# Attention and two feed-forward layers on one core: raw-weight loads one half-step nearer to their first use, and the third block's attention re-timed

## The chip, the cores and the metric

The kernel runs on one core of a Trainium2 chip. The metric is the device time of one execution in microseconds (us), smaller is better. The engines are PE (TensorE matmul; PEld its weight loads), DVE (VectorE), ACT (ScalarE), POOL (GpSimd) and SP (SyncE, which here only issues transfers).

## The reference, cut to what matters

```python
scores = (q @ k^T) / 8                 # 4 batches, 8 heads, 576 tokens, head size 64
# heads 0-3: a query sees its last 32 keys; heads 4-7: every 4th key of its last 128
attn = softmax(where(mask, scores, -1e9))
x = (attn @ v) as (2304 tokens, 512)
h = x @ w_in                           # 512 x 2048
y = where(h > 0, h, exp(min(h, 0)) - 1) @ w_out
out = ((y @ w_a) * (y @ w_b)) @ w_out2 # 512 x 1536, 1536 x 512
```

All inputs are float32, and the weights reach the core as raw 64-bit words (two halves each), from which the kernel assembles the float32 number with some vector work.

## The kernel before, in words

**Two stages.** The tokens are cut into six blocks `t` = 0 to 5 of 384. The first stage computes the first feed-forward layer in 96 steps; a step `s` is one (block, 128-column chunk of w_in) pair from the list `STEPS1`: steps 0 to 6 are block 0, 7 to 22 block 1, 23 to 31 the rest of block 0, and from 32 on 16 steps for each of blocks 2 to 5. The second stage computes the second layer in twelve big steps (`ab_step`, L974 and L1290).

**One step.** In the main loop (`for s in range(NS1)`) a step runs, in this order: slot L (transfers), `h1_mm(s)` (12 matmuls of w_in, L525, then the negated relu and the exp of it on ACT, L546 and L547), slots A0 and A, `h1_g(s)` (DVE joins the two, L552; ACT and POOL split the result in a high and a low part, L536 and L537), slot C, `y1_mm(s - 2)` (12 matmuls of w_out, L571), slots B, B2, B3, C2. So the second product follows its own first product by two steps. `ps_h`, the result of L525, has two buffers, so `h1_mm(s)` needs L552 of step `s - 2` to be done.

**Attention, block by block.** A block's four head pairs `p` (0, 1 plain, 2, 3 dilated) are computed some steps before the block's own steps: q and k are loaded (`att_load`, L335, three buffers `qk`), then v (`att_load_v`, L349, two buffers), then scores (`att_scores`, L474: both heads' results in the two buffers of the PSUM pool `ps_a`), softmax of head 0 and of head 1 one step later (mask added by DVE L490, maximum L356, exp on ACT L360, scaled by POOL L370), transposes (`att_transpose`, L499, each into a `ps_a` buffer, copied out by ACT, L502), and the product with v (`att_values`, L514, again a `ps_a` buffer; ACT L462 and DVE L463 make `x` of it). Which step each happens in is a table: `B1` for block 1, `B2` for block 2, and a formula for the later ones; `end` is the step of the transposes. Block 2 is the third block.

**Background work.** The rest of w_in and w_out and all weights of the second layer are assembled from raw words between the steps: `unit_ops` and `chunk_ops` list operations (`Op`), and `tick`, called twice a step (slots C and A0: a half-step), hands out those that are ready, within a room for each engine. A chunk is loaded (`load`, L866, into one of four `wraw` buffers), then ACT runs `high` and `low` (L252, L257), DVE the rest (L262, L267, L270), DVE forms sums (L917), ACT and DVE split them (L278, L901), and SP and ACT store them to DRAM (L829), from which the second stage fetches them (L651). `Op.ready` (L773) holds an operation back until those before it were handed out some half-steps ago. For the first operation on a loaded chunk this is `LAG_IN`; `first` is true in the first 32 half-steps (steps 7 to 22), and from half-step `LATE` = 146 (step 80) on `LAG_LATE` = 7 holds:

```python
C1, C0, AHEAD, LAG_IN, LAG_OUT = SPLIT, NF1 + SPLIT, 56, 4, 2
...
                    lag = LAG_IN - first if now[0] < LATE else LAG_LATE
                    lag = lag if x.takes else 2
```

The order of instructions on an engine is fixed when the program is built. ACT, DVE, POOL and SP run theirs one after another, so an operation that waits holds up all behind it.

Of the kernel before, what the change touches and what calls it, by code (L numbers as in the profile page):

```python
# [22 lines left out]
B, H, S, D = 4, 8, 576, 64  # L23
# [8 lines left out]
NP = H // 2  # L32
KC = DM // 128
NF1, NF2 = F1 // 128, F2 // 128


SPLIT = 7
# [13 lines left out]
Y2_LAG = 6  # L51


C1, C0, AHEAD, LAG_IN, LAG_OUT = SPLIT, NF1 + SPLIT, 56, 4, 2
LATE, LAG_LATE = 2 * (NF1 * (NB - 1) - C1), 7

ROOM1 = {"V": 1.8, "A": 1.4, "G": 0.9}
# [6 lines left out]
ON3 = {"a": ("AV",) * 4, "b": ("AV",) * 4, "o": ("AV",) * 4}  # L64
CV0, CV1, LAG = 3, 8, 3
B1 = (-4, -2, 0, 2)
B2 = (18, 21, 23, 26)
EARLY = 2
UE = {False: (64, 6), True: (48, 8)}
LP, LD = TB + WIN, NU * UK  # L70
# [145 lines left out]
def banded_attention_two_ffn(ctx: ExitStack, tc: tile.TileContext, ins, out):  # L216
    nc = tc.nc
    V, A, G, T, SP = nc.vector, nc.scalar, nc.gpsimd, nc.tensor, nc.sync
# [366 lines left out]
    def y1_mm(s):  # L585
        for part in y1_parts(s):
            part()
# [117 lines left out]
    def y2_steps(S):  # L705

        first, rest = [], []
        for op, i in (("11", 0), ("21", 1)):
            first += [(y2_tiles, S, op), (y2_load, S, op, i, 0)]
        first += [(int,)] * Y2_LAG  # L710
        for op in ("11", "21"):
            first.append((y2_split, S, op, "AA", "VV"))
        rest += [(y2_temp, S, "t3"), (y2_load, S, "t3", 0, 1)]
        rest += [(y2_tiles, S, "22"), (y2_load, S, "22", 1, 1)]
        rest += [(y2_temp, S, "t1"), (y2_load, S, "t1", 0, 0)]
        rest += [(y2_sum, S, "t1", "t3", "t1")]
        rest += [(y2_temp, S, "t2"), (y2_sum, S, "t2", "22", "t1")]
        rest += [(y2_tiles, S, "t2"), (y2_split, S, "t2", "AA", "VV")]
        rest += [(y2_tiles, S, "t1"), (y2_split, S, "t1", "AA", "VV")]
        rest += [(y2_sum, S, "t3", "22", "t3")]  # L720
        rest += [(y2_temp, S, "t4"), (y2_load, S, "t4", 1, 0)]
        rest += [(y2_tiles, S, "t3"), (y2_split, S, "t3", "AA", "VV")]
        rest += [(y2_sum, S, "t4", "t4", "t2")]
        rest += [(y2_tiles, S, "t4"), (y2_split, S, "t4", "AA", "VV")]
        rest += [(y2_split, S, "22", "AA", "VV"), (y2_t.clear,)]
        return first, rest
# [39 lines left out]
    ops, room, now = [], {"A": 0.0, "V": 0.0, "G": 0.0}, [0]  # L766
    n_free = {"wraw": NRAW, "wt": 4}

    class Op:
# [6 lines left out]
        def ready(self):  # L776
            for x in self.after:
                if x.at is None:
                    return False
                first = now[0] <= 2 * (C0 - C1)  # L780
                if x.eng == "D":
                    lag = LAG_IN - first if now[0] < LATE else LAG_LATE
                    lag = lag if x.takes else 2
                elif self.gives and first:
                    lag = 0
                elif self.eng == "D":
                    lag = self.lag if self.fn else 1
                else:
                    lag = int(x.eng != self.eng)
                if x.at + lag > now[0]:  # L790
                    return False
            if self.takes and n_free[self.takes] <= 0:
                return False
            return self.eng == "D" or room[self.eng] >= 0
# [527 lines left out]
    def at_step(step, slot, fn, *args):  # L1322
        todo.setdefault((step, slot), []).append((fn, args))

    def run(step, slot):
        for fn, args in todo.pop((step, slot), ()):
            fn(*args)
# [25 lines left out]
    first = steady.tile([128, 4], F32, "nm")  # L1353
# [17 lines left out]
    for i in range(len(seq) + 4):  # L1371
        if i < len(seq):
            p, b = seq[i]
# [9 lines left out]
        if 0 <= i - LAG < len(seq):  # L1383
            p, b = seq[i - LAG]
# [28 lines left out]
    for t in range(1, NB):  # L1413
        for p in range(NP):
            if t == 1:
                b0 = B1[p]
            elif t == 2:
                b0 = B2[p]
            else:
                b0 = NF1 * (t - 1) - 4 + 4 * p  # L1420
            at_step(max(0, b0 - 3), "L", held, att_load, t, p)
            at_step(max(0, b0 - 3) if t < EARLY else b0 + 2, "L", held, att_load_v, t, p)
            if t < EARLY:
                end = b0 + 1 + int(b0 >= 0)
                at_step(max(b0, 0), "A", early_scores, t, p)
                for i in range(2):
                    at_step(max(b0 + i, 0), "A", early_softmax, t, p, i)
                    at_step(max(end + i, 0), "B", early_transpose, t, p, i, A)
                at_step(max(end + 2, 0), "B2", early_values, t, p)
            else:  # L1430
                at_step(b0, "A", att_scores, t, p)
                hurry = t == EARLY and p == NP - 1
                end = b0 + 4 + int(not hurry)
                for i in range(2):
                    at_step(b0 + i, "A", att_softmax, t, p, i)
                    at_step(end, ("B", "B2")[i] if hurry else ("A", "B")[i], att_transpose, t, p, i, A)
                at_step(end + 1, "B2" if hurry else "B", att_values, t, p)
    at_step(6, "L", lambda: SP.dma_start(out=masks, in_=ins["masks"]))

    at_step(NF1 + 13, "L2", held, y_part_load)  # L1440
# [49 lines left out]
    first, rest = y2_steps(0)  # L1490
# [5 lines left out]
    for s in range(NS1):  # L1496
# [7 lines left out]
        if s >= 2:  # L1504
            y1_mm(s - 2)
        for sl in ("B", "B2", "B3", "C2"):
            run(s, sl)
# [68 lines left out]
```

## Time and profile before

| what | value |
|---|---|
| time, median of 3 runs | 928.32 us (927.14 to 930.19) |
| the profiled execution | 928.17 us |
| its span, first to last instruction | 926.3 us |
| busy: PE, PEld, DVE | 903.6, 864.9, 650.9 us |
| busy: ACT, POOL | 522.8, 288.1 us |
| DMA queues q1 and q10 | 55.5% and 5.6% of 16 engines' span |
| L525, L571, L974, L1290 on PE | 224.0, 225.1, 294.1, 154.1 us |

The time and the span differ by 1.9 us of start and end. PE's busy time is counted from the start of a matmul to a modelled end, so two matmuls in a row overlap, and a busy PE can still run below its best rate: what a group takes is read from its start to the start of the next group. "Idle before" in a row is time in which the engine stood still, with what ended it.

### The profile page before, as it was taken

To read this page: it belongs to the slowest core of one execution; us is meant where nothing else is said; L and a number is where in the kernel's file an instruction comes from. 1 tells how busy PE (TensorE), PEld (TensorE's weight loads), DVE (VectorE), ACT (ScalarE), POOL (GpSimd) and SP (SyncE) were. 2 spreads that over 40 slices of the span, in tenths; PEclk is the share of its full clock that TensorE was granted. 3 is DMA by queue.
4 is the path that set the end of the run, shared out by engine and by line. 5 is a ranking of instruction groups with operands and counts; after the bars stand their busy time and mean duration, and the time that the engine had idled before them with its cause. 6 is when DMAs were issued, how large, how long until landed. Compare 5 with 4: busy or idle time off the path is not lost. (4 is left out here: it accounts for less than half of the span.)

```text
span 926.3 us, 17004 instructions
## 1 busy us (share of the span) xinstructions
PE 903.6 (98%) x6155; PEld 864.9 (93%) x6157; DVE 650.9 (70%) x1147; ACT 522.8 (56%) x1328; POOL 288.1 (31%) x260
## 2 busy tenths in 40 slices
PE   9999997999999999999999999999999999999998
PEld 5789987999999999999998999999999999999998
DVE  6898898758656767666775258788746688746566
ACT  6897787776777776776566354224343325342331
POOL 2323233323333323342232132222622222622233
PEclk9999998999999999999999999999999999999999
DMA  9854443557455554535897489884687663686622
GB/s 282 239 207 171 138 154 118 200 157 245 149 173 165 198 179 164 182 137 187 297 345 275 171 278 346 270 302 157 212 336 268 241 224 117 227 324 242 238 70 69
DMA packets 75859, 195.79 MB, mean 211 GB/s; under 512 B 8288, under 2 KB 22240, under 8 KB 75776
## 3 DMA queue, kind: packets, MB, share of 16 engines
q1 hardware_dynamic: 63680, 175.70, 55.5%
q10 hardware_dynamic: 12096, 19.01, 5.6%
q8 instruction: 49, 0.80, 0.3%
q14 instruction: 34, 0.28, 0.1%
HBM read 151.16 MB, written 43.52 MB: 210 GB/s over the span
## 5 line engine op out<-in xcount | busy, mean ns | idle before, releaser
L974 PE MATMUL ps_h<-y,w 128*128 128x384 f32 x1512 | 294.1, 337 | 2.5 <-DVE el L1029 1.1
L974 PEld LDWEIGHTS ps_h<-y,w 128*128 128x128 f32 x1512 | 255.9, 188 | 6.6 <-DVE el L1029 2.0
L525 PE MATMUL ps_h<-x,w 128*128 128x384 f32 x1152 | 224.0, 341 | 5.5 <-DVE el L552 3.9
L571 PE MATMUL ps_y<-g,w 128*128 128x384 f32 x1152 | 225.1, 341 | 3.2 <-ACT w L278 1.4
L525 PEld LDWEIGHTS ps_h<-x,w 128*128 128x128 f32 x1152 | 198.5, 188 | 12.9 <-DVE el L552 6.5
L571 PEld LDWEIGHTS ps_y<-g,w 128*128 128x128 f32 x1152 | 200.4, 189 | 8.4 <-ACT el L608 1.8
L537 POOL TENSOR_TENSOR g<-el,g 128x384 fp32r<-128x384 f32 x96 | 118.7, 1236 | 276.8 <-ACT g L536 236.6
L1290 PE MATMUL ps_o<-w,g 128*128 128x256 f32 x1071 | 154.1, 282 | 0.4 <-ACT g L1090 0.4
L1290 PEld LDWEIGHTS ps_o<-w,g 128*128 128x128 f32 x1071 | 147.4, 188 | 1.3 <-ACT g L1090 0.9
L552 DVE SCALAR_TENSOR_TENSOR el<-el,ps_h 128x384 f32<-128x384 f32 x96 | 52.9, 551 | 90.3 <-ACT el L547 89.6
L1016 POOL TENSOR_TENSOR g<-el,g 128x384 fp32r<-128x384 f32 x34 | 39.4, 1160 | 120.5 <-ACT g L1015 105.6
L1313 DVE TENSOR_TENSOR acc<-acc,ps_o 128x512 f32<-128x512 f32 (+1 forms) x77 | 49.6, 644 | 32.0 <-PE ps_o L1290 31.6
L536 ACT ACTIVATE g<-el 128x384 fp32r<-128x384 f32 x96 | 49.9, 520 | 28.6 <-DVE el L552 27.1
L546 ACT ACTIVATE el<-ps_h 128x384 f32<-128x384 f32 x96 | 46.3, 482 | 33.6 <-PE ps_h L525 27.2
L370 POOL TENSOR_TENSOR e<-e,rs 96x512 f32<-96x512 f32 (+2 forms) x40 | 40.3, 1007 | 54.7 <-DVE rs L369 44.0
L267 DVE SCALAR_TENSOR_TENSOR wt<-wt,wraw 128x512 uint32<-128x512 uint32 x68 | 53.9, 796 | 2.8 <-ACT wraw L257 1.3
L270 DVE SCALAR_TENSOR_TENSOR wt<-wraw,wt 128x512 uint32<-128x512 uint32 x68 | 53.9, 798 | 0.6
L547 ACT ACTIVATE el<-el 128x384 f32<-128x384 f32 x96 | 50.2, 523 | 1.6
L257 ACT ACTIVATE wraw<-wraw 128x512 uint32<-128x512 uint32 x68 | 44.8, 668 | 10.4 <-DMA wraw<-in_w2b 6.9
L360 ACT ACTIVATE e<-e,nm 96x128 f32<-96x128 f32 x128 | 49.8, 392 | 1.5 <-ACT nm L358 1.0
L252 ACT ACTIVATE wt<-wraw 128x512 f32<-128x512 f32 x68 | 44.8, 665 | 5.4 <-DMA w2Q__5915<-wt 2.0
L1064 DVE TENSOR_TENSOR u<-ps_h,u 128x384 f32<-128x384 f32 x36 | 20.0, 556 | 36.2 <-PE ps_h L974 36.2
(111 smaller groups left out, 1071.0 us busy)
## 6 DMA issues: line engine op xcount, KB each, us to landing
w<-w2P_o SPq DMA_DIRECT2D x52, 512.0 KB, 5.6
w<-w2P_a SPq DMA_DIRECT2D x48, 512.0 KB, 4.5
w<-w2P_b SPq DMA_DIRECT2D x48, 512.0 KB, 4.3
wraw<-in_w1i SPq DMA_DIRECT2D x16, 512.0 KB, 4.3
wraw<-in_w1o SPq DMA_DIRECT2D x16, 512.0 KB, 3.3
wraw<-in_w2a SPq DMA_DIRECT2D x12, 512.0 KB, 3.6
wraw<-in_w2b SPq DMA_DIRECT2D x12, 512.0 KB, 4.2
wraw<-in_w2o SPq DMA_DIRECT2D x12, 512.0 KB, 4.2
```

The costliest lines, as they stand in the source:

```text
L267: V.scalar_tensor_tensor(t, t, 3, L, op0=ALU.logical_shift_left, op1=ALU.bitwise_or)
L270: V.scalar_tensor_tensor(t, H, 0x80000000, t, op0=ALU.bitwise_and, op1=ALU.bitwise_or)
L360: A.activation(e[:, i], sc[:, i], AF.Exp, bias=nm[:, i : i + 1], scale=scale, accum_out=sm[:, i : i + 1],)
L525: T.matmul(ps[:, :TB], w[:, wi, kc * 128 : (kc + 1) * 128], xs[kc][:, xi, :], start=(n == 0), stop=(n == 3 * KC - 1),)
L536: A.activation(g[:, 0, :], gf, AF.Copy)
L537: G.tensor_tensor(g[:, 1, :], gf, f32(g[:, 0, :]), op=ALU.subtract)
L547: last_e[0] = A.activation(e, e, AF.Exp, scale=-1.0)
L552: last_g[0] = V.scalar_tensor_tensor(e, e, -1.0, h_ps.pop(s)[:, :TB], op0=ALU.add, op1=ALU.max)
L571: T.matmul(y_ps[t][c][:, :TB], w[:, wi, c * 128 : (c + 1) * 128], g[:, gi, :], start=(first and n == 0), stop=(last and n == 2),)
L974: last_mm[0] = T.matmul(ps[:, :TB], w[:, wi, kc * 128 : (kc + 1) * 128], y2[S, yop][kc][:, xi, :], start=(start and n == 0), stop=(n == 5) ...
L1290: T.matmul(ps[:, 256 * n : 256 * n + 256], g[name][:, gi, i * 128 : (i + 1) * 128], w[:, wi, h, :], start=((first or not held) and n == m ...
L1313: V.tensor_tensor(a, a, ps[:, :n], op=ADD)
```

## The change

```diff
-C1, C0, AHEAD, LAG_IN, LAG_OUT = SPLIT, NF1 + SPLIT, 56, 4, 2
+C1, C0, AHEAD, LAG_IN, LAG_OUT = SPLIT, NF1 + SPLIT, 56, 3, 2
...
-B2 = (18, 21, 23, 26)
+B2, B3 = (18, 21, 24, 27), (29, 32, 36, 40)
...
-                    lag = LAG_IN - first if now[0] < LATE else LAG_LATE
+                    lag = LAG_IN if now[0] < LATE else LAG_LATE
...
                 b0 = B2[p]
+            elif t == 3:
+                b0 = B3[p]
...
                 at_step(b0, "A", att_scores, t, p)
-                hurry = t == EARLY and p == NP - 1
-                end = b0 + 4 + int(not hurry)
+                end = b0 + 5 if t > EARLY else (23, 26, 28, 30)[p]
                 for i in range(2):
                     at_step(b0 + i, "A", att_softmax, t, p, i)
-                    at_step(end, ("B", "B2")[i] if hurry else ("A", "B")[i], att_transpose, t, p, i, A)
-                at_step(end + 1, "B2" if hurry else "B", att_values, t, p)
+                    at_step(end, ("A", "B")[i] if t > EARLY else ("B", "B2")[i], att_transpose, t, p, i, A)
+                at_step(end + 1, "B" if t > EARLY else "B2", att_values, t, p)
```

`EARLY` is 2, so the new branch is for block 2. What it does:

- Half-steps 33 to 145 (steps 23 to 79): a chunk's first operation is handed out from three half-steps after its load, not four. Steps 7 to 22 have three in both, steps from 80 on seven.
- Block 2, pairs 2 and 3: q/k load, scores, softmax and v load one step later. The steps of their transposes (28 and 30) stay.
- Block 2, pairs 0 to 2: both heads' transposes behind `y1_mm` of their step, where head 0's stood ahead of it; the product with v in slot B2 of the next step, not B. Pair 3 had these slots already.
- Block 3 (the fourth), pair 0: all of it one step later (28 to 29).

**PE, steps 23 and 24** (L525 of step 23 first; L499 are the transposes of pair 0, L474 the scores of pair 2, L514 the product with v of pair 0). Before:

```order
L525 MATMUL ps_h<-x,w 128x384 x12
L499 MATMUL ps_t<-ident,e 128x96 x4
L474 MATMUL ps_s<-qk 96x128 x4
L571 MATMUL ps_y<-g,w 128x384 x4
L474 MATMUL ps_s<-qk 96x128 x4
L571 MATMUL ps_y<-g,w 128x384 x8
L499 MATMUL ps_t<-ident,e 128x96 x4
L525 MATMUL ps_h<-x,w 128x384 x12
L571 MATMUL ps_y<-g,w 128x384 x12
L514 MATMUL ps_v<-pt,v 64x96 x8
```

Now:

```order
L525 MATMUL ps_h<-x,w 128x384 x12
L571 MATMUL ps_y<-g,w 128x384 x12
L499 MATMUL ps_t<-ident,e 128x96 x8
L525 MATMUL ps_h<-x,w 128x384 x12
L474 MATMUL ps_s<-qk 96x128 x8
L571 MATMUL ps_y<-g,w 128x384 x12
L514 MATMUL ps_v<-pt,v 64x96 x8
```

The transposes moved behind a whole L571, and the scores of pair 2 behind the next L525. (A trace counts L474 and L514 twice, so x4 here is x8 there.)

**ACT, the same place** (L546 is the relu of step 23, L502 the copies of pair 0's transposes). Before:

```order
L252 ACTIVATE wt<-wraw 128x512
L368 ACTIVATE rs<-sm 96x4
L546 ACTIVATE el<-ps_h 128x384
L502 COPY pt<-ps_t 128x384
L547 ACTIVATE el<-el 128x384
L278 ACTIVATE wraw<-wraw 128x512
L829 DMA w2P_0_a<-wraw 128x512
L358 ACTIVATE nm<-nm 96x4
L536 ACTIVATE g<-el 128x384
L360 ACTIVATE e,sm<-e,nm 96x128 x4
L502 COPY pt<-ps_t 128x384
```

Now:

```order
L252 ACTIVATE wt<-wraw 128x512
L368 ACTIVATE rs<-sm 96x4
L546 ACTIVATE el<-ps_h 128x384
L278 ACTIVATE wraw<-wraw 128x512
L547 ACTIVATE el<-el 128x384
L829 DMA w2P_0_a<-wraw 128x512
L536 ACTIVATE g<-el 128x384
L502 COPY pt<-ps_t 128x384 x2
L829 DMA w2P_0_a<-wraw 128x512
L546 ACTIVATE el<-ps_h 128x384
```

All ahead of L546 is unchanged. Both copies now stand together, behind L278, L547 and L536; the exp of pair 2 (L358, L360) moved away from here.

**ACT, the last raw chunk of the program** (its L252, the first operation on it). Before, in the second stage:

```order
L1038 COPY u<-ps_h 128x384
L1310 COPY acc<-ps_o 128x512
L252 ACTIVATE wt<-wraw 128x512
L1045 COPY u<-ps_h 128x384
L1310 COPY acc<-ps_o 128x256
```

Now, in the first stage, ahead of the relu of step 91:

```order
L829 DMA w2P_5_b<-wt 128x512
L252 ACTIVATE wt<-wraw 128x512
L546 ACTIVATE el<-ps_h 128x384
L278 ACTIVATE y_5985<-yt 128x384
L547 ACTIVATE el<-el 128x384
```

The background work, with shorter periods between its loads, ends some steps earlier.

## Rows read from the trace of the kernel before

**Rows 1.** Busy us by stretch: PE, PEld, DVE, ACT, POOL, clock, DMA share, GB/s

```profile
143.00:154.00 11.00, 6.27 (x39) 5.59 (x37) 10.41 (x20) 9.67 (x34) 3.95 (x3) 0.91 0.32 118
154.00:164.00 10.00, 9.90 (x56) 9.28 (x58) 6.38 (x15) 6.36 (x26) 3.79 (x3) 0.76 0.35 120
200.00:445.00 245.00, 244.10 (x1673) 233.26 (x1673) 163.70 (x291) 175.63 (x499) 80.83 (x71) 1.00 0.53 178
```

**Rows 2.** PE in order of time, steps 23 to 32: start, us, instruction, idle before

```profile
144.66 2.27 PE L525 MATMUL ps_h<-x,w 128*128 128x384 f32 x12
...
148.91 0.96 PE L571 MATMUL ps_y<-g,w 128*128 128x384 f32 x4
154.10 2.02 PE L474 MATMUL ps_s<-qk 64*96 64x128 f32 x8 [4.22 <-ACT pt L502]
156.05 2.93 PE L571 MATMUL ps_y<-g,w 128*128 128x384 f32 x8
...
163.46 0.88 PE L514 MATMUL ps_v<-pt,v 128*64 128x96 f32 x16
...
171.04 1.80 PE L474 MATMUL ps_s<-qk 64*96 64x128 f32 x16
...
183.59 1.63 PE L474 MATMUL ps_s<-qk 64*96 64x128 f32 x16 [0.27 <-DVE x L463]
```

**Rows 3.** PE, undisturbed: scores of one pair, and a step late in the first stage

```profile
225.52 1.12 PE L474 MATMUL ps_s<-qk 64*96 64x128 f32 x16
...
473.25 2.24 PE L571 MATMUL ps_y<-g,w 128*128 128x384 f32 x12
475.33 2.24 PE L525 MATMUL ps_h<-x,w 128*128 128x384 f32 x12
```

**Rows 4.** ACT in order of time, step 23

```profile
153.22 0.47 ACT L546 ACTIVATE el<-ps_h 128x384 f32<-128x384 f32 x1
153.59 0.46 ACT L502 COPY pt<-ps_t 128x384 f32<-128x384 f32 x1
...
153.94 0.52 ACT L547 ACTIVATE el<-el 128x384 f32<-128x384 f32 x1
154.37 0.62 ACT L278 ACTIVATE wraw<-wraw 128x512 fp32r<-128x512 f32 x1
...
156.07 0.52 ACT L536 ACTIVATE g<-el 128x384 fp32r<-128x384 f32 x1 [0.31 <-DVE el L552]
```

**Rows 5.** DVE in order of time, steps 22 and 23

```profile
149.53 0.55 DVE L552 SCALAR_TENSOR_TENSOR el<-el,ps_h 128x384 f32<-128x384 f32 x1 [0.45 <-ACT el L547]
...
153.72 0.42 DVE L917 TENSOR_TENSOR wraw<-wt,wraw 128x256 f32<-128x256 f32 x1
```

**Rows 6.** ACT, steps 88 to 91 and the second stage: waits of the background work

```profile
486.93 0.67 ACT L257 ACTIVATE wraw<-wraw 128x512 uint32<-128x512 uint32 x1 [2.23 <-DMA wraw<-in_w2b]
...
501.09 0.66 ACT L252 ACTIVATE wt<-wraw 128x512 f32<-128x512 f32 x1 [2.05 <-DMA w2Q__5915<-wt]
...
551.15 0.66 ACT L252 ACTIVATE wt<-wraw 128x512 f32<-128x512 f32 x1 [0.93 <-DMA w2P_b<-wt]
```

**Rows 7.** PE at the same places

```profile
489.24 2.35 PE L525 MATMUL ps_h<-x,w 128*128 128x384 f32 x12 [0.87 <-DVE el L552]
...
502.88 1.31 PE L525 MATMUL ps_h<-x,w 128*128 128x384 f32 x6 [0.88 <-DVE el L552]
...
552.23 2.38 PE L974 MATMUL ps_h<-y,w 128*128 128x384 f32 x12 [0.52 <-ACT u L1045]
```

**Rows 8.** A raw load on SP's queue, its first operation on ACT; loads of 200 to 445 us

```profile
238.23 1.03 SPq L866 DMA_DIRECT2D wraw<-in_w2o  x2
...
245.00 0.67 ACT L252 ACTIVATE wt<-wraw 128x512 f32<-128x512 f32 x1
...
wraw<-in_w2b SPq DMA_DIRECT2D x8, 512.0 KB, 4.2
```

**Rows 9.** L552, once a step: count, first and last start

```profile
L552 DVE SCALAR_TENSOR_TENSOR el<-el,ps_h x96: 534/554/556, 32.7 to 510.8; 128x384 f32<-128x384 f32 x96
```

## The prediction

> **What bounds the kernel now.** I read the busy times by stretch first, then PE's instructions in order of time, then those of ACT and DVE around PE's longest stop, then SP's loads. From 200 to 445 us PE is busy 244.1 of 245 us [rows 1], so the middle of the first stage has nothing to win: a change there can only cost. Two kinds of place are left. One is step 23, where PE stands 4.22 us for an ACT copy of the transposes, L502, before it can go on with scores [rows 2]. The same stretch shows ACT busy 9.67 and DVE 10.41 of 11 us [rows 1]: these two are the bound there, PE runs ahead of them. The granted clock is 0.91 of full over these 11 us and 0.76 over the next 10 [rows 1]; with 0.5 as the low level (1.2 of 2.4 GHz), that is 2.0 + 4.8 = 6.8 us at the low level, beginning in PE's idle stretch. The other kind is three stops of 0.5 to 0.9 us late in the first stage and early in the second [rows 7], each just behind an ACT operation on raw weights that itself waited for a transfer [rows 6].
>
> **The third block's attention.** The change puts more PE work ahead of the scores of pair 2, so one might expect the stop to go. I replay it on the new order.
>
> PE: L525 of step 23 starts at 144.66 as before [rows 2]. Twelve matmuls take 475.33 - 473.25 = 2.08 us when nothing is in the way [rows 3]. L525, then the whole L571, end at about 148.9; eight transposes bring it to 149.5. L525 of step 24 needs L552 of step 22, which ends at 149.53 + 0.55 = 150.1 [rows 5], and is through at 152.2. Now the scores need both `ps_a` buffers, hence both copies.
>
> ACT: up to L546 at 153.22 [rows 4] its order and DVE's are the same as before, so that time stands. Then comes L278, which reads sums that DVE's last L917 finishes at 153.72 + 0.42 = 154.1 [rows 5]; L278 0.62, L547 0.52, DVE's L552 0.55, L536 0.52 [rows 4, 5] give 156.3 to 156.4, and two copies of 0.46 end at 157.3. If L278 needs only the sums before the last, it is 156.9. I take 157.2.
>
> So PE waits from 152.2 to 157.2, 5.0 us against 4.2 before. The copy that held PE up moves behind more of ACT's queue, and **the stop stays**. What is gained is that PE stops with more behind it. From 154.10 to 163.46 PE did half the scores, 8 of L571, the second transposes, L525 and L571 [rows 2]. In the new order only the scores (1.12, [rows 3]) and L571 of step 22 (2.08) are left at 157.2. At the low clock PE lost about 2.8 us: half the scores took 156.05 - 154.10 = 1.95 where half of 1.12 is usual, 8 of L571 2.93 where 8/12 of 2.24 is [rows 2, 3]. If it loses as much again, it is at the product with v at 157.2 + 1.1 + 2.1 + 2.8 = 163.2, against 163.46: 0.3 us gained.
>
> Further gains come behind it. The scores of pair 3 took 1.80 and those of the next block's pair 0 1.63 after a wait of 0.27, each where 1.12 is usual [rows 2, 3]: 0.7 + 0.5 + 0.3 = 1.5 us. In the new order a whole L525 stands between a pair's transposes and the next scores, over 2 us for two copies of 0.46, and ACT no longer has pair 2's exp in its queue ahead of them; I take all 1.5. The last of the gain is at step 32, where L525 needs x of pair 3; I take 0.4, from the shorter queue ahead of L462. **Sum: 2.2 us**, with bounds of 0.7 (only half of the 1.5, nothing else) and 2.7.
>
> The transfers that move with pairs 2, 3 and 0 are their q, k and v on SP. In SP's order a store of weights (L829) now goes ahead of a q/k load that waits for pair 2's scores, instead of behind it, and the v loads stay behind the same products. All of them are used steps later, on a PE that is full there: nothing.
>
> **The lag.** From four half-steps to three, each pair of raw loads takes one half-step less: by the half-steps in which the planner hands them out, a unit of six loads takes 24 instead of 27. In the middle stretch ACT is busy 175.6 and DVE 163.7 of 245 us [rows 1]; a tenth more of their background part stays beside PE's work and costs nothing while the loads land in time.
>
> Do they? A step is (510.8 - 32.7) / 95 = 5.03 us [rows 9], a half-step 2.5. A load that was planned four half-steps ahead went out at 238.23, and its L252 ran at 245.00, 6.8 us later; landing takes 4.2 us [rows 8]. One half-step less leaves 4.3, no margin. But in the new order L252 regularly stands behind the exp (L547) of its step rather than ahead of the relu, which gives some of it back. I take zero; the ends are zero and the price of the rival on late loads below. The Trainium skill, page "DMA: Bandwidth & Descriptors", section "Rules for kernel authors", speaks against this part: issue a transfer early and wait for it late. By that rule the sum would be the late-load rival's. The trace agrees only so far that a late load does stop ACT, for 2.23 us at 486.93 [rows 6].
>
> What the lag does buy is the end. The last chunk's L252 moves from the second stage (551.15) to step 91. PE's stop of 0.52 at 552.23 stands right behind it [rows 6, 7], so 0.5 us goes. The stops of 0.87 and 0.88 follow a late raw load and a buffer whose store was late [rows 6, 7]; seven half-steps hold there as before, but the pattern shifts, and I count half: 0.9. **Sum: 1.4 us**, bounds 0 and 2.3 (all three).
>
> **Total.** The profiled execution took 928.17 us, close to the median of 928.32. 928.17 - 2.2 - 1.4 = 924.6; I forecast **924.5 us**. By the bounds of both sums this case runs from 923.2 to 927.5. About 0.3% (2.8 us) is what a measurement of this kernel can tell from no change.
>
> **Rivals.**
>
> *The clock stays up.* The stop is there, but the clock doesn't fall in it. Idle of about 1 us, as before L525 at 489.24, went by at full clock; 4.2 us did not. The new stop of 5.0 us is no shorter, which speaks against. Price: 2.8 us more, 924.5 - 2.8 = 921.7. The Trainium skill, page "TensorE: Matmul & The Clock Gate", section "What's actually happening", says that the gate looks at activity in windows that run freely, not from the start of an idle stretch; by it a stop that begins 2.4 us later can fall otherwise. No run here shows a second such stop.
>
> *The stop goes.* If ACT's copies came through soon after the transposes, PE would not wait. The sources are ready by 149.5; against it stands the order on ACT, which puts L278, L547 and L536 first. Price: 5.0 + 2.8 more, 924.5 - 7.8 = 916.7.
>
> *Given back.* The stop is as long as before, the pairs behind it gain only the low end, 0.7, and the two waits for transfers at the end return at other steps. Then 928.17 - 0.7 - 0.5 = 927.0. For it speaks that ACT and DVE are the bound at step 23 and no work leaves them.
>
> *Slower: raw loads land late.* By the planner's half-steps some 14 of the loads between steps 24 and 79 have only three. If they land after 4.3 us, ACT stops in front of L536 and holds up all behind it. At 486.93 a stop of 2.23 us cost PE 0.87 [rows 6, 7]. It decides once landing passes 4.3 us, against 4.2 now [rows 8]; 1.3 us late on each would cost 14 x 1.3 x 0.87 / 2.23 = 7 us, so 928.17 - 2.2 + 7 = 933. Against it: ACT has 70 of 245 us idle, and PE's own lead of two steps takes up short stops.
>
> **Chances.** Forecast 0.42, clock up 0.14, stop gone 0.08, given back 0.28, late loads 0.08. Faster by over 0.3% means under 925.5: the forecast but for 0.03, and the first two rivals, 0.61. Within 0.3%: 0.31. Slower: 0.08. The range takes in the forecast, the clock's rival and the one given back with 1.5 us beyond, and leaves out the far ends: 919.0 to 928.6.
>
> **What would show it.** Right: in PE's order of time an idle stretch of about 5 us ahead of the scores of pair 2, ended by L502, later than before by 2 to 3 us; a stretch at the low clock behind it; scores of pair 3 and of the next pair 0 at about 1.1 us; no L252 in the second stage; ACT's waits for raw loads in the middle no more than before. Wrong: no such stop, a clock of 1.00 throughout, or ACT waiting for raw loads time after time between 200 and 445 us with PE stops behind.

## The result and the profile after

The changed kernel takes 918.06 us (median of 4 runs, 917.34 to 918.62) where the kernel before, beside it on the same chip, took 927.73 us: a ratio of 0.9894 (95% interval 0.9875 to 0.9913). That is 9.7 us faster where 3.7 was forecast, and 0.9 us below the range. The profiled run took 918.29 us, its span is 916.3 us against 926.3. PE runs 6155 instructions in both traces, and ACT's busy time stays (522.8 to 523.5 us): no work has gone. PE's busy time, which counts matmuls to a modelled end, falls from 903.6 to 898.2 us.

**Where the 10.0 us went.** Both traces, PE in order of time: L525 of step 40, then the first matmul of L525 of step 81 and of step 95 (start, us, instruction). The kernel before:

```profile
243.03 2.25 PE L525 MATMUL ps_h<-x,w 128*128 128x384 f32 x12
...
444.04 0.35 PE L525 MATMUL ps_h<-x,w 128*128 128x384 f32 x1
...
507.32 0.34 PE L525 MATMUL ps_h<-x,w 128*128 128x384 f32 x1
```

The changed kernel:

```profile
241.77 2.25 PE L525 MATMUL ps_h<-x,w 128*128 128x384 f32 x12
...
441.53 0.35 PE L525 MATMUL ps_h<-x,w 128*128 128x384 f32 x1
...
500.10 0.34 PE L525 MATMUL ps_h<-x,w 128*128 128x384 f32 x1
```

The first L525 starts at 18.26 us where before had 17.70, 0.56 later, in a part of the program that the change doesn't touch. From there to step 40, where the tables of attention no longer differ, the changed kernel gains 1.26 + 0.56 = 1.82 us, to step 81 another 2.51 - 1.26 = 1.25, over the 14 steps from 81 to 95 it gains 63.28 - 58.57 = 4.71, and from there to the end (926.3 - 507.32) - (916.3 - 500.10) = 2.78. In all 1.82 + 1.25 + 4.71 + 2.78 - 0.56 = 10.00.

**Third block, PE** in order of time (start, us, instruction, idle before it), the answer to [rows 2]:

```profile
150.72 2.35 PE L525 MATMUL ps_h<-x,w 128*128 128x384 f32 x12 [0.46 <-DVE el L552]
156.97 2.40 PE L474 MATMUL ps_s<-qk 64*96 64x128 f32 x16 [3.90 <-ACT pt L502]
159.30 4.21 PE L571 MATMUL ps_y<-g,w 128*128 128x384 f32 x12
163.44 0.89 PE L514 MATMUL ps_v<-pt,v 128*64 128x96 f32 x16
```

**ACT**, the same place, the answer to [rows 4]:

```profile
154.31 0.63 ACT L278 ACTIVATE wraw<-wraw 128x512 fp32r<-128x512 f32 x1
...
154.84 0.51 ACT L547 ACTIVATE el<-el 128x384 f32<-128x384 f32 x1
156.03 0.52 ACT L536 ACTIVATE g<-el 128x384 fp32r<-128x384 f32 x1 [0.68 <-DVE el L552]
...
156.46 0.84 ACT L502 COPY pt<-ps_t 128x384 f32<-128x384 f32 x2
```

The stop is there, 2.9 us later, behind the queue that was replayed: L278, L547, L552, L536, two copies. L474 and L571 behind it take about twice their 1.12 and 2.24 us: the low clock again (0.90 in the mean from 140 to 175 us, shown at the end). The two copies end at 156.46 + 0.84 = 157.30, so the scores started behind the first of them and not behind both, as was replayed.

**The late steps**, busy us by stretch (PE, PEld, DVE, ACT, POOL, clock, DMA share, GB/s), steps 81 to 95. Before:

```profile
444.00:507.30 63.30, 60.66 (x338) 58.05 (x337) 47.69 (x78) 40.42 (x84) 18.14 (x13) 1.00 0.87 316
```

Changed:

```profile
441.50:500.10 58.60, 58.60 (x338) 58.30 (x337) 46.58 (x73) 38.07 (x79) 15.62 (x13) 1.00 0.90 329
```

PE is full now: 58.57 us for 14 steps are 4.18 a step, two undisturbed groups of 2.08 [rows 3]. Before, the same 338 records cost 4.7 us more; 2.6 of it shows as PE not busy (63.30 - 60.66), the rest lies inside groups that only look busy.

**ACT's waits for transfers**, the groups of L252 and L257 between 200 and 600 us: count, min/median/max ns, first and last start, and for what ACT stood idle ahead of them (us, times). Before:

```profile
L252 ACT ACTIVATE wt<-wraw x29: 642/659/686, 216.8 to 551.2; 128x512 f32<-128x512 f32 x29
  DMA w2Q__5915<-wt: 2.0, 1
  DMA w2P_a<-wt: 1.1, 1
  DMA w2P_b<-wt: 0.9, 1
...
  DMA wraw<-in_w2b: 6.9, 3
  DMA wraw<-in_w2o: 0.9, 1
```

Changed:

```profile
L252 ACT ACTIVATE wt<-wraw x29: 645/649/675, 215.4 to 488.4; 128x512 f32<-128x512 f32 x29
...
  DMA wraw<-in_w2o: 0.4, 1
```

This is the reading that the prediction had the wrong way round: with a shorter lag ACT waits less for transfers, 0.4 us in place of 11.8, and the last first operation starts at 488 us, no longer in the second stage.

### The profile page after: what moved, and what is told of

Read it like the earlier page. It is cut to its first block, busy times and chain, and to the rows that moved or that the text cites. A ratio compares the mean times of both kernels' runs of the same rounds, so it can differ in the third digit from the quotient of the medians.

```text
span 916.3 us, 17034 instructions
## 1 busy us (share of the span) xinstructions
PE 898.2 (98%) x6155; PEld 863.2 (94%) x6157; DVE 660.0 (72%) x1147; ACT 523.5 (57%) x1328; POOL 283.0 (31%) x260
## 4 chain that ended last, share of the span: by engine, by line
PE 78%; DVE 6%; ACT 2%; issue 1%; DMA 0%; ACTq 0%; DVEq 0%; SPq 0%
PE ps_h L974 27%; PE ps_y L571 17%; PE ps_h L525 16%; PE ps_o L1290 13%; PE ps_s L474 2%; PE ps_v L514 1%; PE ps_t L499 1%; PE ps_o L1150 1%; DVE wt L267 1%; DVE wt L262 1%; DVE wt L270 1%; ACT e L360 0%; DVE w L854 0%; DVE u L1082 0%; DVE wraw L917 0%
## 5 line engine op out<-in xcount | busy, mean ns | idle before, releaser
L525 PE MATMUL ps_h<-x,w 128*128 128x384 f32 x1152 | 223.5, 340 | 4.6 <-DVE el L552 2.2
L571 PE MATMUL ps_y<-g,w 128*128 128x384 f32 x1152 | 224.2, 341 | 2.0 <-ACT w L278 1.4
L525 PEld LDWEIGHTS ps_h<-x,w 128*128 128x128 f32 x1152 | 198.8, 188 | 10.8 <-DVE el L552 3.6
L571 PEld LDWEIGHTS ps_y<-g,w 128*128 128x128 f32 x1152 | 201.2, 189 | 5.7 <-ACT w L278 1.8
L537 POOL TENSOR_TENSOR g<-el,g 128x384 fp32r<-128x384 f32 x96 | 115.5, 1203 | 276.1 <-ACT g L536 243.6
L552 DVE SCALAR_TENSOR_TENSOR el<-el,ps_h 128x384 f32<-128x384 f32 x96 | 52.9, 552 | 81.7 <-ACT el L547 80.8
L1016 POOL TENSOR_TENSOR g<-el,g 128x384 fp32r<-128x384 f32 x34 | 38.8, 1140 | 121.6 <-ACT g L1015 106.7
L546 ACT ACTIVATE el<-ps_h 128x384 f32<-128x384 f32 x96 | 46.5, 484 | 42.1 <-PE ps_h L525 38.1
L267 DVE SCALAR_TENSOR_TENSOR wt<-wt,wraw 128x512 uint32<-128x512 uint32 x68 | 63.0, 930 | 3.8 <-ACT wraw L257 1.3
L270 DVE SCALAR_TENSOR_TENSOR wt<-wraw,wt 128x512 uint32<-128x512 uint32 x68 | 61.2, 904 | 0.9
L536 ACT ACTIVATE g<-el 128x384 fp32r<-128x384 f32 x96 | 49.6, 516 | 16.8 <-DVE el L552 16.7
L547 ACT ACTIVATE el<-el 128x384 f32<-128x384 f32 x96 | 50.1, 522 | 1.8
L360 ACT ACTIVATE e<-e,nm 96x128 f32<-96x128 f32 x128 | 49.8, 391 | 1.0 <-ACT nm L358 0.3
L257 ACT ACTIVATE wraw<-wraw 128x512 uint32<-128x512 uint32 x68 | 45.0, 667 | 3.8 <-DMA wraw<-in_w1i 1.6
L1025 ACT COPY el<-ps_h 128x384 f32<-128x384 f32 x36 | 17.2, 479 | 50.3 <-PE ps_h L974 48.0
```

The costliest lines, as they stand in the source:

```text
L267: V.scalar_tensor_tensor(t, t, 3, L, op0=ALU.logical_shift_left, op1=ALU.bitwise_or)
L270: V.scalar_tensor_tensor(t, H, 0x80000000, t, op0=ALU.bitwise_and, op1=ALU.bitwise_or)
L360: A.activation(e[:, i], sc[:, i], AF.Exp, bias=nm[:, i : i + 1], scale=scale, accum_out=sm[:, i : i + 1],)
L525: T.matmul(ps[:, :TB], w[:, wi, kc * 128 : (kc + 1) * 128], xs[kc][:, xi, :], start=(n == 0), stop=(n == 3 * KC - 1),)
L536: A.activation(g[:, 0, :], gf, AF.Copy)
L537: G.tensor_tensor(g[:, 1, :], gf, f32(g[:, 0, :]), op=ALU.subtract)
```

## The experiments

The theories at the start: (A) late in the first stage PE loses because raw-weight operations on ACT wait for a transfer and hold up the g behind them ("position"); (B) it loses because the background still runs there, and into the second stage ("end"). Columns of the table: median time, ratio to the kernel before in the same session with its 95% interval, ACT's idle time ahead of L252 and L257 that a transfer ended (200 to 600 us), the last start of L252, the time from L525 of step 81 to that of step 95, and from there to the end of the span.

| run | us | ratio | waits | last L252 | 81 to 95 | rest |
|---|---|---|---|---|---|---|
| before | 928 to 930 | 1 | 11.8 | 551 | 63.3 | 419.0 |
| changed | 918.06 | 0.9894 (0.9875-0.9913) | 0.4 | 488 | 58.6 | 416.2 |
| e1 | 920.81 | 0.9903 (0.9880-0.9925) | 0.5 | 490 | 59.2 | 416.2 |
| e2 | 926.81 | 0.9980 (0.9964-0.9996) | 13.7 | 549 | 61.6 | 418.0 |
| e3 | 921.16 | 0.9910 (0.9884-0.9937) | 9.4 | 537 | 60.6 | 417.0 |
| e4 | 916.68 | 0.9857 (0.9836-0.9879) | 0.6 | 487 | 59.8 | 416.0 |
| e5 | 918.87 | 0.9873 (0.9847-0.9900) | 7.0 | 542 | 59.5 | 419.0 |
| e6 | 928.18 | 0.9986 (0.9968-1.0004) | 31.5 | 502 | 62.1 | 416.3 |
| e7 | 917.34 | 0.9855 (0.9826-0.9884) | 0.9 | 486 | 59.6 | 416.2 |
| e8 | 925.21 | 0.9946 (0.9924-0.9968) | 8.7 | 498 | 59.6 | 416.7 |
| c1 | 918.56 | 0.9887 (0.9866-0.9908) | 0.3 | 488 | 58.8 | 416.2 |
| e10 | 923.39 | 0.9944 (0.9927-0.9962) | 6.9 | 496 | 60.2 | 416.3 |
| e11 | 926.49 | 0.9972 (0.9958-0.9987) | 33.0 | 505 | 61.2 | 416.2 |
| e9 | 910.91 | 0.9810 (0.9788-0.9832) | 0.2 | 480 | 58.7 | 416.5 |

### e1 and e2: each half alone

e1 is the kernel before with the lag alone, e2 with the tables of attention alone.

```diff
# e1
-C1, C0, AHEAD, LAG_IN, LAG_OUT = SPLIT, NF1 + SPLIT, 56, 4, 2
+C1, C0, AHEAD, LAG_IN, LAG_OUT = SPLIT, NF1 + SPLIT, 56, 3, 2
-                    lag = LAG_IN - first if now[0] < LATE else LAG_LATE
+                    lag = LAG_IN if now[0] < LATE else LAG_LATE
# e2: all other lines of the change
```

> The lag of three half-steps alone, attention tables as before. Theory A (the two parts add, and what the changed kernel gained from 436 us on, 7.2 us by the starts of L552 and L1064, is the lag's): 928 - 7 to 8 = 920 to 921 us; step 23's stop of 4.2 us on L502 and the scores of 1.8 and 1.6 us are there as before. Rival (the late gain needs the third block's earlier finish): no better than 925.

> The attention tables and slots alone, lag of four half-steps. Theory A: 928 - 2 to 3 = 925 to 926 us, with the stop of about 4 us ahead of the scores of pair 2, the late stops between 445 and 590 us as before, and the last L252 in the second stage. Rival: below 922, the late stops gone too because the steps fall otherwise.

The lag alone gives 8.2 us (928.97 to 920.81), the tables alone 2.2. The two add up to the whole, within a microsecond. The third block's term, forecast at 2.2, fits; the lag's, forecast at 1.4, does not. That the tables alone gave just 2.2 is in part luck: e2's trace is 2.8 us shorter than before's, but only 1.3 of it is gained from step 0 to step 40; it gains 0.1 more to step 81 and 1.7 and 1.0 in the two late columns, and starts 1.3 later.

### e3 and e8: the end moved, back and forth

e3 is the changed kernel with no raw load handed out in half-steps 83 to 95; e8 the kernel before, lag of four kept, with `LAG_OUT` 1.

```diff
# e3
+            if self.takes == "wraw" and 82 < now[0] < 96:
+                return False
# e8
-C1, C0, AHEAD, LAG_IN, LAG_OUT = SPLIT, NF1 + SPLIT, 56, 4, 2
+C1, C0, AHEAD, LAG_IN, LAG_OUT = SPLIT, NF1 + SPLIT, 56, 4, 1
```

> The changed kernel, but no raw load is handed out in half-steps 83 to 95, so that the last raw chunk is as late as before (its first operation at half-step 178, before 180, changed 169). Theory 1 (the gain is where the background work ends): it gives the late gain back, 924 to 926 us, with PE stops between 445 and 590 us. Theory 2 (the gain is the even rhythm that a lag of three half-steps gives, L252 and L257 behind the exp): 918 to 920 us, no more than 1 us of stops there.

> The kernel before, with LAG_OUT 1 in place of 2 (the sums, splits and stores of a unit one half-step earlier) and the lag of four half-steps kept; the planner's last work then ends ten half-steps earlier, as far as in the changed kernel, with the loads still four half-steps ahead. Theory 'end': most of the late gain comes, 921 to 923 us. Theory 'position': the first operations of the late steps fall where the new pattern puts them, ahead of L536 in about half of the cases, and the time stays at 925 to 929 us.

e3 gives back 1.5 to 3 us (by the ratios 0.991 and 0.989, whose intervals overlap, and by the medians 921.2 and 918.1), which lies between its two forecasts; in its trace 2.0 us of it are lost between steps 81 and 95 and 0.8 behind, and the waits return to 9.4 us. e8's 925.21 lies in the range of theory "position", at its edge, but the columns are plainer: with the lag of four, steps 81 to 95 take 59.6 and the rest 416.7, 3.7 and 2.2 us better than before; it loses 2.1 us of that between steps 22 and 81 (by the starts of L525). So a late part nearly as good as the changed kernel's is to be had without the shorter lag. In all runs the last column goes with the last L252: 416.0 to 416.7 where it starts by 505 us, 417.0 at 537, 418.0 to 419.0 from 542 on. **That much, 2.8 us of the gain, is the end.**

### e5: other places on ACT, the same end

```diff
-                after = last_e if behind_exp and x.eng == "A" else last_g
+                after = last_e if x.eng == "A" else last_g
```

> The kernel before, with every background operation of ACT placed behind the step's last exp or behind its g, never ahead of L536 of its own step; lag and tables as before. Theory 'position' (late in the first stage PE loses because raw-weight operations of odd half-steps stand ahead of L536 and wait there for a transfer): the 7.2 us of the late part come back in good part, 923 to 925 us, and between 436 and 600 us the stops of PE ahead of L525 go. Theory 'end' (PE loses there because the background work still runs in the last steps of the stage, four half-steps of lag making each unit of loads longer): the end doesn't move, so no gain over 1 us, 927 to 929 us.

The planner's half-steps are untouched, and so is the rest: 419.0 us. But the 14 steps fall from 63.3 to 59.5. **So 3.8 us of the 4.7 between steps 81 and 95 are to be had from later places of the same operations alone**, with the end where it was. e5 was not to go below 923; it is at 918.87 because it also gains 4.3 us up to step 34 (3.5 of it by step 22, by the starts of L525), which neither theory spoke of: there the background now lies behind the exp too, and PE's waits for L552 between 80 and 140 us, 1.7 us in the kernel before, are gone; that is part of it.

### e6, e10 and e11: the same rhythm, shifted

With lag three the raw loads go out every four half-steps, each unit in step with the attention pairs, which come every four steps. The three runs shift this rhythm by one, two and three half-steps against the changed kernel; c1 is the changed kernel word for word, beside e10 and e11.

```diff
# e6
+            if self.takes == "wraw" and now[0] == 53:
+                return False
# e10 (e11: != 0)
+            if self.takes == "wraw" and 52 < now[0] < 146 and now[0] % 4 != 3:
+                return False
```

> The changed kernel, with one raw load held back for one half-step (no load is handed out in half-step 53), so that all later first operations fall on the other half of a step; the end moves by one half-step only. Theory 'position': the L252 of the late steps stand ahead of L536 again and the stops return, 3 to 7 us slower than the changed kernel, 921 to 925 us. Theory 'end': under 0.5 us, 917.5 to 919 us.

> The changed kernel once more, word for word, so that the other three have it beside them on the same chip. About 918 us, 0.988 to 0.991 of the kernel before.

> The changed kernel, with raw loads between half-steps 53 and 145 held to every fourth one, one whole step later than in the changed kernel: same rhythm of four steps, first operations on the same half of a step, one step later against the attention pairs; the end two half-steps later. Theory 'half of the step' (a first operation behind the exp finds its data, one ahead of L536 waits for it): ACT's waits for transfers between 200 and 600 us stay under 2 us and the time stays within 1.5 us of the changed kernel. Theory 'place against the attention pairs' (what counts is which of the four steps of a pair the load meets): ACT waits as in the kernel before, 3 us or more lost. Theory 'end': 0.3 us lost for each half-step of the end, as with the run that held back the late loads, 0.6 us here, so this theory and the first differ little here and are told apart by the next run.

> The same with the loads three half-steps later than in the changed kernel: first operations on the other half of a step, and the end three half-steps later. Theory 'half of the step': ACT waits for transfers some 20 us in all between 200 and 600 us, as in the run shifted by one half-step, and the time is 6 to 10 us over the changed kernel. Theory 'place against the pairs': it can go either way, but not as the run shifted by one and the run shifted by two both do. Theory 'end': 1 us lost.

One half-step of one load, and of all behind it, costs 9 to 10 us: e6 is as slow as the kernel before, slower than both theories forecast, with 31.5 us of waits on ACT. e11, on the same half of a step, is 7.9 us over c1 with 33.0 where some 20 were expected; 3.7 us of it go at one place, step 36, where the new rhythm sets in (its rows stand in the last section). e10 is back on the good half; its waits are 6.9, more than the 2 of the forecast, and it is 4.8 us over c1, where under 1.5 was expected. Its trace says why. PE in order of time:

```profile
335.20 0.38 PE L514 MATMUL ps_v<-pt,v 128*64 128x96 f32 x2
335.51 0.44 PE L525 MATMUL ps_h<-x,w 128*128 128x384 f32 x1
335.89 0.88 PE L514 MATMUL ps_v<-pt,v 128*64 128x96 f32 x14
336.69 2.17 PE L525 MATMUL ps_h<-x,w 128*128 128x384 f32 x11
338.70 2.24 PE L571 MATMUL ps_y<-g,w 128*128 128x384 f32 x12
```

The changed kernel, the same pieces of another step:

```profile
295.72 0.88 PE L514 MATMUL ps_v<-pt,v 128*64 128x96 f32 x16
296.53 2.37 PE L525 MATMUL ps_h<-x,w 128*128 128x384 f32 x12
298.74 1.55 PE L571 MATMUL ps_y<-g,w 128*128 128x384 f32 x8
```

In e10 a matmul of L525 was put between the first product with v and the others when the program was built: 338.70 - 335.20 = 3.50 us against 298.74 - 295.72 = 3.02. That, or in two cases four matmuls of L525 and a whole L571 in between, happens eight times between 275 and 416 us; by the starts of L525 it costs 0.5 us each, 4.1 in all, without any wait. It is all that e10 loses from step 34 to step 81 (233.7 us, c1 229.6). Why the pieces are slower in this order is not shown. The 0.7 us that are left are within what was expected of the half. So a shifted table can move more than the waits, and the order that PE got has to be looked at too.

What the half of a step does shows in one place. All engines in order of time, the changed kernel:

```profile
309.07 0.33 SPq L866 DMA_DIRECT2D wraw<-in_w2a  x1
...
319.16 0.53 ACT L547 ACTIVATE el<-el 128x384 f32<-128x384 f32 x1
319.59 0.65 ACT L252 ACTIVATE wt<-wraw 128x512 f32<-128x512 f32 x1
...
320.71 0.51 ACT L536 ACTIVATE g<-el 128x384 fp32r<-128x384 f32 x1
```

e6, the same chunk (its line numbers are two higher from L793 on):

```profile
314.81 0.33 SPq L868 DMA_DIRECT2D wraw<-in_w2a  x1
...
315.69 0.43 SPq L831 DMA_DIRECT2D w2Q__3674<-wt  x1
...
318.21 0.51 ACT L547 ACTIVATE el<-el 128x384 f32<-128x384 f32 x1
...
320.12 0.66 ACT L252 ACTIVATE wt<-wraw 128x512 f32<-128x512 f32 x1 [1.40 <-DMA w2Q__3674<-wt]
...
321.24 0.51 ACT L536 ACTIVATE g<-el 128x384 fp32r<-128x384 f32 x1
```

Theory A falls in the form in which it was written down (that L252 stands ahead of the g in one case and not in the other): it stands between exp and g in both, and so does every L252 of e6 between 200 and 440 us that waited for a transfer, though 13 of its 24 stand elsewhere. What differs is how long its transfers have had. In the changed kernel the load went out 10.5 us ahead of it, in e6 5.3, and there the store that empties its `wt` buffer, the one that it waits for, only 4.4. Waits for the loads themselves come at L257, 16.0 of e6's 31.5 us. Then ACT stands, the g behind it is late, and PE falls behind: from step 34 to step 81 it takes 234.5 us where the changed kernel takes 229.6. "Three half-steps" in the plan is thus 10.5 us or 5.3 on the chip.

This holds beyond the one chunk. With the 28 loads that go out between 200 and 600 us paired in order with their L252 and L257, the first use comes less than 5 us after the issue at 13 loads in e6 and in e11, at 2 in e10, the kernel before and e3, at 3 in e2, 4 in e8, and at none in the changed kernel, c1, e1, e4, e5, e7 and e9. So e5 does not part places from time: its later places also give every load 6.5 us or more.

### e4, e7 and e9: the stop at step 24, and a kernel that beats both

e4 is the changed kernel with the scores of pair 2 at step 25; e7 with pair 1's scores at step 22 and pair 0 transposed at 21; e9 is e7 with ACT's background behind the exp in steps 7 to 22 as well.

```diff
# e4
-B2, B3 = (18, 21, 24, 27), (29, 32, 36, 40)
+B2, B3 = (18, 21, 25, 27), (29, 32, 36, 40)
-                at_step(end + 1, "B" if t > EARLY else "B2", att_values, t, p)
+                at_step(end + 1 + int(t == EARLY and p == 0), "B" if t > EARLY else "B2", att_values, t, p)
# e7
+B2, B3 = (18, 22, 24, 27), (29, 32, 36, 40)
+                end = b0 + 5 if t > EARLY else (21, 26, 28, 30)[p]
# e9: e7 and
+                early = now[0] <= 2 * (C0 - C1)
+                after = last_e if (behind_exp or early) and x.eng == "A" else last_g
```

> The changed kernel with the scores of the third block's pair 2 at step 25, not 24, and pair 0's product with v one step later too. If the stop is the wait for copies that stand behind ACT's queue until 157.3 us, a PE that has L571 and L525 to do first reaches the scores at about 157 to 158: a wait of at most 1.5 us, no stretch at the low clock, 918 - 5 to 6 = 912 to 913 us. Rival (ACT and DVE are the bound, and the time is lost a step later): 917 to 918 us.

> The changed kernel, with pair 0 of the third block transposed at step 21 (its product with v at 22) and pair 1's scores at step 22, so that the scores of pair 2 at step 24 need no fresh copy. If PE's stop there is a matter of where ACT's copies stand: no stop of 3.9 us at 157, none above 2 us in its place, no stretch at the low clock, 3 to 5 us faster than the changed kernel, 913 to 915 us. If ACT and DVE are the bound over steps 20 to 30 however the pairs are placed: the idle time of PE turns up at another step, in smaller pieces, and the time stays within 1.5 us of the changed kernel, 917 to 919 us.

> A kernel meant to beat both: the changed one with pair 0 of the third block transposed at step 21, and with the background operations of ACT placed behind the step's exp in steps 7 to 22 as well. In the run with all of them behind the exp, step 22 was 5.5 us earlier than before, and 2.7 us of it went again by step 34 under the old table. If that gain and the one of the transposes at step 21 hold side by side: 910 to 913 us. If ACT's copies at steps 20 to 24 come later again because the background is now behind the exp there: 915 to 918 us.

PE's longest stop of that region, in e4:

```profile
163.73 0.88 PE L514 MATMUL ps_v<-pt,v 128*64 128x96 f32 x16 [2.77 <-DVE e L490]
```

In e7:

```profile
145.30 1.49 PE L474 MATMUL ps_s<-qk 64*96 64x128 f32 x16 [2.24 <-ACT pt L502]
```

In e9, the same stop and a second one:

```profile
140.07 1.49 PE L474 MATMUL ps_s<-qk 64*96 64x128 f32 x16 [0.85 <-ACT pt L502]
...
166.86 1.48 PE L474 MATMUL ps_s<-qk 64*96 64x128 f32 x16 [1.30 <-ACT pt L502]
```

In e4 the scores no longer wait, and the product with v does, for a buffer. In e7 the stop is shorter and the clock stays at 1.00 from 140 to 175 us. Both stand at a ratio of 0.986 where the changed kernel, in other sessions, has 0.989: some 1 to 3 us, less than the 3 to 6 expected: the stop moves before it shrinks. In e7 and e9 ACT's copies still end it; in e4 it is DVE's L490, which reads earlier scores out of the buffer that the product needs. In e9 that stop is down to 0.85 us, another of 1.30 comes up, and the gain is what was forecast for it: 910.91 us, against c1's 918.56 and 929.58 before in the same session. It beats both kernels.

## Why the prediction was wrong

By its own steps:

- **The third block: right in its mechanism.** Stop of 5.0 us from 152.2 to 157.2, ended by L502: the scores started at 156.97, after a wait of 3.90. It is shorter than forecast because L525 ahead of them came 0.6 us later than replayed (150.72 for 150.1, as late as the whole program started) and its modelled end lies another 0.3 on (2.35 for 2.08), and the scores came 0.2 sooner, behind one copy and not two. Product with v forecast for 163.2: 163.44. From the scores to there the low clock cost 6.47 - 3.2 = 3.3 us where 2.8 were priced; the rival "the clock stays up" did not happen here. The scores of pair 3 (at 175.55) and of the next pair 0 (at 187.69) took 1.12 us, as forecast. The sum, 2.2, measured 2.5 at step 34 (L525 at 211.97 for 213.90, and 0.56), of which 0.7 is lost again by step 40: steps 34 and 35 are 0.5 us longer in every run with the new tables, most likely by the fourth block's later pair, which the prediction put at nothing; no run moves that pair alone.
- **The lag, middle: zero forecast, 1.25 us gained.** The fear was that three half-steps leave 4.3 us and no margin. The step that failed there is the arithmetic "6.8 us less one half-step": it took one load of the old pattern for the new one, whose loads between 200 and 440 us all have 9.1 us or more. Its premise failed too, that PE at 244.1 busy us of 245 has nothing to win. The waits of 6.6 us on ACT that before has between 200 and 440 us are gone, among them one of 3.29, behind which ACT is late until L608 and PE stops for 0.86 us:

```profile
286.50 0.66 ACT L257 ACTIVATE wraw<-wraw 128x512 uint32<-128x512 uint32 x1 [3.29 <-DMA wraw<-in_w2b]
...
296.88 0.45 PE L571 MATMUL ps_y<-g,w 128*128 128x384 f32 x1 [0.86 <-ACT el L608]
```

  (The kernel before.) The rival on late loads rests on the same arithmetic; what it describes is e6 and e11, not the changed kernel. The Trainium skill, page "DMA: Bandwidth & Descriptors", section "Rules for kernel authors", says to issue early and wait late. The runs agree once the distance is read from the trace: 10.5 us ahead without a wait; 5.3 us for the load, and 4.4 for the store, with one of 1.4. What misled was to read it off the plan's lag.
- **The lag, late end: 1.4 forecast (2.3 at most), 7.5 measured, 4.7 in steps 81 to 95 and 2.8 behind.** This is the step that failed and made the total wrong: the direction was right, the size was not. It added up the idle time of three rows [rows 7] and halved two. But the 14 steps could have been held against 14 x 4.16 = 58.2 us, two groups of 2.08 [rows 3]: before took 63.3, so 5.0 us lay there to be had, of which those two rows show 1.75. The average step of 5.03 us [rows 9] does not show it, since these steps have no attention on PE and can be 0.9 us shorter. And the chunk in the second stage was priced at one stop of 0.52, where the whole stage was 2.8 us longer with it.

What stays open: how the 4.7 us divide. Places alone give 3.8 (e5), an earlier end with lag four gives 3.7 (e8), so the two overlap, and a wait can be taken away by either. Single traces of the late part may also scatter: e2, with no change to the lag, gains 1.7 in these steps, while the changed kernel and c1 differ by 0.2.

## What to carry to other kernels

Hold every stretch of the bound engine against its undisturbed pace, start to start, before pricing single stops: idle time in rows shows only part of what is lost. A lag in a planner's units says nothing on the time that a transfer gets; read from the trace when it goes out and when it is used, and where the background has the same period as the foreground try every phase of it, since one half-step here was worth as much as the whole change.

## What the runs showed of the hardware

The granted clock after like stops was not alike. In e2 and in the changed kernel PE did the same (a stop of 3.88 and 3.90 us in front of the same scores), and the mean clock from 140 to 175 us was 0.95 in the one and 0.90 in the other. Two views of e2, first PE in order of time:

```profile
159.17 2.40 PE L474 MATMUL ps_s<-qk 64*96 64x128 f32 x16 [3.88 <-ACT pt L502]
161.50 3.03 PE L571 MATMUL ps_y<-g,w 128*128 128x384 f32 x12
164.46 0.88 PE L514 MATMUL ps_v<-pt,v 128*64 128x96 f32 x16
```

Then the stretch (busy us of PE, PEld, DVE, ACT, POOL, clock, DMA share, GB/s):

```profile
140.00:175.00 35.00, 30.82 (x201) 29.24 (x201) 31.29 (x54) 27.84 (x83) 14.88 (x13) 0.95 0.49 167
```

The changed kernel:

```profile
140.00:175.00 35.00, 30.64 (x186) 29.24 (x185) 30.60 (x52) 26.88 (x82) 12.73 (x11) 0.90 0.46 156
```

With 1.2 of 2.4 GHz as the low level that is 35 x 0.05 / 0.5 = 3.5 us of it against 7: from the start of the scores to the product with v e2 took 164.46 - 159.17 = 5.29 us, the changed kernel 163.44 - 156.97 = 6.47, so the same stop cost 1.2 us more behind it in one program than in the other. The Trainium skill, page "TensorE: Matmul & The Clock Gate", section "What's actually happening", says that the gate's windows run freely; two like stops with unlike low stretches agree with that. The length of a stop does not settle it either. In e11, at step 36, a stop of 1.77 us was followed by the low clock (PE, then the stretch behind it):

```profile
225.87 1.11 PE L474 MATMUL ps_s<-qk 64*96 64x128 f32 x14 [1.77 <-DVE x L463]
226.91 3.91 PE L571 MATMUL ps_y<-g,w 128*128 128x384 f32 x12
...
227.00:231.00 4.00, 4.00 (x14) 4.00 (x15) 3.71 (x7) 2.94 (x11) 1.31 (x1) 0.57 0.83 263
```

In e7 a longer stop, of 2.24 us, was not:

```profile
140.00:175.00 35.00, 32.47 (x228) 30.09 (x228) 32.55 (x58) 28.57 (x86) 14.49 (x12) 1.00 0.55 172
```

A forecast of the cost of such a stop has to carry more than one value.
